# Second MoE by Winograd products: gate weights loaded a step earlier, output weights streamed for each pair of token blocks, one sum of z at a time, three output tiles

## The chip, the cores and the metric

The kernel runs on one core of one Trainium2 chip (one core, one launch). The metric is the device time of one execution in microseconds. Every profile here is one profiled execution of that one core. Engines are named as in the profile: PE multiplies, PEld loads its weights, DVE, ACT and POOL are the three elementwise engines, SP issues all DMAs.

## What is computed

The reference is a chunked attention followed by two feed-forward layers, all in fp32:

```python
x = attention(q, k, v, mem_k, mem_v)            # 4 x 768 tokens, 8 heads of 64 -> 3072 x 512
x = (np.maximum(x @ w_in, 0.0) ** 2) @ w_out    # first MoE: 512 -> 2048 -> 512
g = x @ w_gate                                  # second MoE: 512 -> 1536
out = (g / (1.0 + np.exp(-g)) * (x @ w_val)) @ w_out2    # 1536 -> 512
```

The weights arrive as float64; the kernel makes fp32 of them. An fp32 operand of a matmul is split in two parts, `hi` (rounded by ACT) and `lo` (the rest, by POOL or DVE), and each product is the sum of hi·hi, hi·lo and lo·hi.

## The kernel before

The program has two stages. Until about 629 us it does attention and the first MoE, in 8 blocks of 384 tokens and 16 slices of w1, with attention laid between. During that stage the second MoE's weights are turned into fp32, combined for the Winograd form and stored in two DRAM buffers, `w2g` (gate and value, 7 pieces for each of 12 slices f, L66) and `w2o` (output weights, two slices at a time, L67). The result of the first MoE goes to DRAM as `y1d`.

The change is in the second stage. It has 48 steps: 4 blocks s of 768 tokens, and for each the 12 slices f (`seq2`, L480). One step i is a call of `gated` (L417): seven products of 6 matmuls with 384 columns, L405, called A11, S2, A12, S3, S1, A22, S4. Each is read out of `hbank` by an ACT copy (L421) or a DVE operation (L425 to L449). Between them `fill` lays the 18 matmuls with 512 columns of `output` of the step before (L468). The results are combined by DVE L438 to L451 and ACT `Silu` (L430, L450), and rounded to `uh`, `ul` (L412 to L415), which the next step's `output` reads. PE's order is the order of the program. The other engines' instructions are ordered by a scheduler, within what the buffers allow.

What has to be ready for a step:
- its gate weights. `load_gv(i, half)` issues a DMA of 512 or 384 KB into a buffer of the tag "cut" (two buffers, `CB`, L32), `split_gv` casts it on ACT and subtracts on POOL, into a pair of buffers of the pool `wp`. Loads of step i+1 are put in slots 1 and 2 of step i, their splits in slots 3 and 5 (L580).
- the output weights. `load_out(c)`, `split_out(c)` bring the six pairs of slices in while s is 0; they stay in 12 of the 32 buffers of `wp` to the end (dictionary `wo`).
- z, the tokens of the block s in the forms that Winograd needs. `load_z` (L358) reads `y1d` into two buffers "raw"; `split_b1` splits B11 and B21 into the tile `z`; `sums_1` and `sums_2` form T1, T3, T2, T4 on POOL (L379, L380, L386, L387, 128x768 each); `split_t` splits the five forms into pairs of `wp` by halves of 384 columns. The forms of the next s are made in the last steps of the present one, four of the five in step 11 (L586 to L589).

`wp` has 32 buffers, 16 pairs. During the first MoE they hold w1 and come free as its last block uses them.

At f = 11 `output` finishes each of six tiles in turn, copies it to SBUF by ACT (L474) or DVE (L472) into one of two buffers "o" (L470) and stores it (L476).

The lines of the loads in the schedule, before the change:

```python
for slot, fn, half in ((1, load_gv, 0), (2, load_gv, 1), (3, split_gv, 0), (5, split_gv, 1)):
    job(i, slot, fn, i + 1, half)
if i % 2 == 0 and i // 2 + 1 < NF2 // 2:
    job(i, 6, load_out, i // 2 + 1)
    job(i + 1, 6, split_out, i // 2 + 1)
```

## Time and profile before

| | us |
|---|---|
| median of 3 runs | 1235.07 (1233.87 to 1235.35) |
| the profiled execution's own time | 1234.65 |
| its span, first to last instruction | 1232.8 |
| PE busy | 1164.0 |
| DVE busy | 690.4 |
| ACT busy | 593.5 |
| POOL busy | 320.3 |
| mean granted TensorE clock | 0.989 |

The span is 1.85 us shorter than the execution's own time; that rest lies around the span. The execution is 0.42 us below the median. Busy times of engines overlap, so they do not add up to the span; what an engine's idle time costs depends on whether the engine that ends last was waiting for it.

### The profile page before, as it was taken

How to read it: one execution, taken by the hardware profiler on the slowest of the kernel's cores; microseconds unless marked ns; L12 is line 12 of the kernel's file. 1: busy time of each engine (PE TensorE's matmuls, PEld its weight loads, DVE VectorE, ACT ScalarE, POOL GpSimd, SP SyncE). 2: the span in 40 equal slices, each digit the busy share in tenths (PEclk: the TensorE clock that was granted, in tenths of full speed). 3: DMA queues.
4: the chain of work that ended last, by engine and by line, in shares of the span. 5: the costliest groups of instructions: out<-in, count | busy, mean ns of one | idle time of the engine just before them, and what ended most of it. 6: DMA issues, size and time to landing. Idle time of an engine off the chain costs nothing.

```text
span 1232.8 us, 20450 instructions
## 1 busy us (share of the span) xinstructions
PE 1164.0 (94%) x8000; PEld 1099.2 (89%) x8000; DVE 690.4 (56%) x1251; ACT 593.5 (48%) x1510; POOL 320.3 (26%) x277
## 2 busy tenths in 40 slices
PE   2699999999999999999989999799997999999997
PEld 1599999999999999999988899699896998989896
DVE  7997345547365464532335555645566555665554
ACT  5686545546555554544743334434344333444422
POOL 0000000203011020002446533635335453345510
PEclk9999999999999999999989999899998999999999
DMA  7553205527244452501353122522225222143301
GB/s 269 195 207 117 75 25 173 193 70 273 81 150 147 137 210 80 181 1 69 95 166 95 60 77 77 192 66 68 77 61 192 73 61 90 61 146 103 103 1 51
DMA packets 46848, 140.77 MB, mean 114 GB/s; under 512 B 4512, under 2 KB 14240, under 8 KB 42400
## 3 DMA queue, kind: packets, MB, share of 16 engines
q1 hardware_dynamic: 46752, 139.48, 34.2%
q8 instruction: 62, 1.02, 0.3%
q14 instruction: 34, 0.28, 0.1%
HBM read 112.72 MB, written 26.74 MB: 113 GB/s over the span
## 4 chain that ended last, share of the span: by engine, by line
PE 80%; DVE 8%; DMA 5%; ACT 2%; POOL 2%; issue 2%; SPq 0%; ACTq 0%; DVEq 0%; POOLq 0%
PE hbank L405 25%; PE yb L295 19%; PE hbank L264 19%; PE yb L468 9%; PE abank L468 5%; PE abank L197 2%; POOL wlo L79 2%; DVE pT L178 2%; DMA wraw<-in_w_dram 2%; DMA gvraw<-w2g 1%; PE abank L136 1%; DMA out_dram<-o 1%; DVE wlo L79 1%; DVE cut L97 1%; ACT whi L76 1%
## 5 line engine op out<-in xcount | busy, mean ns | idle before, releaser
L79 POOL TENSOR_TENSOR wlo<-gvraw,whi 128x512 fp32r<-128x512 f32 x192 | 231.4, 1227 | 307.0 <-ACT whi L76 277.0
L264 PE MATMUL hbank<-x,whi 128*128 128x384 f32 x1024 | 200.0, 336 | 0.6 <-ACT x L76 0.6
L264 PEld LDWEIGHTS hbank<-x,whi 128*128 128x128 f32 x1024 | 180.5, 189 | 1.0 <-ACT x L76 0.9
L274 DVE TENSOR_TENSOR gl<-r,gh 128x384 fp32r<-128x384 f32 x128 | 75.1, 588 | 188.8 <-ACT r L273 188.4
L76 ACT CAST uh<-tmp 128x384 fp32r<-128x384 f32 x96 | 49.4, 514 | 191.8 <-DVE tmp L444 166.0
L328 POOL TENSOR_TENSOR wraw<-cut 128x256 f32<-128x256 f32 x24 | 19.8, 848 | 461.3 <-DVE mx L149 342.9
L405 PE MATMUL hbank<-whi 128*128 128x384 f32 x480 | 125.0, 342 | 9.0 <-DVE tmp L439 5.4
L271 ACT ACTIVATE r<-hbank 128x384 f32<-128x384 f32 x128 | 62.9, 491 | 143.2 <-PE hbank L264 142.0
L76 ACT CAST whi<-gvraw 128x512 fp32r<-128x512 f32 x192 | 100.0, 564 | 65.9 <-DMA gvraw<-w2g 38.1
L405 PE MATMUL hbank<-wlo,whi 128*128 128x384 f32 x480 | 125.3, 342 | 0.0
L405 PE MATMUL hbank<-whi,wlo 128*128 128x384 f32 x480 | 123.7, 338 | 0.0
L405 PEld LDWEIGHTS hbank<-whi 128*128 128x128 f32 x480 | 89.8, 190 | 33.0 <-DVE tmp L439 6.5
L295 PE MATMUL yb<-gh,whi 128*128 128x384 f32 x512 | 116.3, 341 | 0.0
L295 PE MATMUL yb<-gh,wlo 128*128 128x384 f32 x512 | 113.5, 335 | 0.0
L295 PE MATMUL yb<-gl,whi 128*128 128x384 f32 x512 | 113.3, 334 | 0.0
L264 PE MATMUL hbank<-x,wlo 128*128 128x384 f32 x512 | 109.6, 334 | 0.0
L178 DVE STREAM_TRANSPOSE pT<-prob 32x256 f32<-32x256 f32 x224 | 97.3, 435 | 3.6
L79 DVE TENSOR_TENSOR ul<-tmp,uh 128x384 fp32r<-128x384 f32 x96 | 66.7, 695 | 45.5 <-ACT uh L76 44.7
L295 PEld LDWEIGHTS yb<-gh,wlo 128*128 128x128 f32 x512 | 91.5, 188 | 0.0
L295 PEld LDWEIGHTS yb<-gh,whi 128*128 128x128 f32 x512 | 89.1, 188 | 2.5
L295 PEld LDWEIGHTS yb<-gl,whi 128*128 128x128 f32 x512 | 90.9, 188 | 0.1
L264 PEld LDWEIGHTS hbank<-x,wlo 128*128 128x128 f32 x512 | 90.7, 188 | 0.0
(92 smaller groups left out, 2042.2 us busy)
## 6 DMA issues: line engine op xcount, KB each, us to landing
wraw<-in_w_dram SPq DMA_DIRECT2D x34, 1024.0 KB, 6.2
gvraw<-w2g SPq DMA_DIRECT2D x48, 512.0 KB, 3.6
gvraw<-w2g SPq DMA_DIRECT2D x48, 384.0 KB, 3.1
qk<-in_att_dram SPq DMA_DIRECT2D x32, 464.0 KB, 4.4
v<-in_att_dram SPq DMA_DIRECT2D x32, 256.0 KB, 3.3
y1d<-ys SPq DMA_DIRECT2D x8, 768.0 KB, 3.8
w2g<-wraw SPq DMA_DIRECT2D x12, 512.0 KB, 3.9
zraw<-y1d SPq DMA_DIRECT2D x8, 768.0 KB, 5.1
```

The lines of the kernel that those rows point to most:

```text
L76: act.copy(hi, src)
L79: lo_engine.tensor_tensor(lo, src, hi.bitcast(F32), ALU.subtract)
L97: dve.scalar_tensor_tensor(w.bitcast(I32), upper, 3, lower, ALU.logical_shift_left, ALU.bitwise_or)
L178: dve.transpose(pT[row:row + 32, :, 32 * c:32 * c + 32], probs[u % 2][32 * c:32 * c + 32, :, col:col + 32],)
L197: pe.matmul(o[r:r + D, h // NI, h % NI // 2], s["v"][:, h * D:(h + 1) * D], pT[:, h], start=True, stop=True, tile_position=(0, r),)
L264: pe.matmul(hps, wt[:, k * 128:(k + 1) * 128], x[:, k, 0:n], start=i == 0, stop=i == 3 * KD - 1)
L271: act.activation(r, hps, AF.Relu)
L274: dve.tensor_tensor(gl, r, gh.bitcast(F32), ALU.subtract)
L295: pe.matmul(y[e], wt[:, c:c + 128], g, start=f == 0 and p == 0, stop=f == NF1 - 1 and p == 2)
L328: pool.tensor_tensor(o, x, y, op)
L405: pe.matmul(to, wt[:, k * 128:k * 128 + 128], z[:, k], start=n == 0, stop=n == 5)
L468: pe.matmul(outs[j], u[:, c:c + 128], wt, start=f == 0 and p == 0, stop=f == NF2 - 1 and p == 2)
```

## The change

Gate weights are loaded almost a step earlier: the loads of step i+1 are put in slots 4 and 7 of step i-1, the splits in slots 2 and 5 of step i. Two buffers "cut" serve only them, since the raw output weights and the temporary t2 now come from `wp` (`spare`). The output weights are no longer kept: they are loaded and split anew for every pair of steps, 24 times in place of 6. B1 is split in two jobs in two steps, sums and splits of z are one a step, and the split of a form is one ACT and one DVE job of 128x768 in place of two of 128x384. Tiles `o` are three. Line numbers behind the diff grow by 5 (L405 becomes L410, L421 becomes L426, L468 becomes L473); sums_1 is L385 and L386, sums_2 L392 and L393.

```diff
@@ -306,7 +306,7 @@
 
     NC2 = NF2 * 3 // 2
     WAT = {n: i * QC for i, n in enumerate(("A11", "A12", "S2", "S3", "S1", "S4", "A22"))}
-    w2t, wo = {}, {}
+    w2t = {}
 
     def load2(c):
         w["raw2", c] = load_w(w2[c])
@@ -330,28 +330,36 @@
         sp.dma_start(out=dst[:, 2 * QC:6 * QC], in_=sums)
         sp.dma_start(out=dst[:, 6 * QC:7 * QC], in_=a22)
 
-    def split_parts(hi, lo, src, n, step, lo_engine):
-        for c in range(0, n, step):
-            split(hi[:, c:c + step], lo[:, c:c + step], src[:, c:c + step], act, lo_engine)
+    def fetch(key, raw, src, n):
+        w["raw2", key] = raw[:, 0:n]
+        sp.dma_start(out=raw[:, 0:n], in_=src)
+
+    def split_w(key):
+        raw = w.pop(("raw2", key))
+        n = raw.shape[1]
+        w2t[key] = pair(wp, "w")
+        for c in (0, n // 2):
+            split(*(t[:, c:c + n // 2] for t in w2t[key]), raw[:, c:c + n // 2], act, pool)
+
+    def spare():
+        return wp.tile([128, WC], F32, tag="w", name="spare")
+
+    NGV = (4 * QC, 3 * QC)
 
     def load_gv(i, half):
-        n = (4 * QC, 3 * QC)[half]
-        w["gv", i, half] = rawp.tile([128, WC], F32, tag="cut", name="gvraw", bufs=CB)[:, 0:n]
         c = 4 * QC * half
-        sp.dma_start(out=w["gv", i, half], in_=w2g[seq2[i][1], :, c:c + n])
+        raw = rawp.tile([128, WC], F32, tag="cut", name="gvraw", bufs=CB)
+        fetch((i, half), raw, w2g[seq2[i][1], :, c:c + NGV[half]], NGV[half])
 
     def split_gv(i, half):
-        w2t[i, half] = pair(wp, "w")
-        n = (4 * QC, 3 * QC)[half]
-        split_parts(*w2t[i, half], w.pop(("gv", i, half)), n, n // 2, pool)
-
-    def load_out(c):
-        w["out", c] = rawp.tile([128, WC], F32, tag="cut", name="oraw", bufs=CB)
-        sp.dma_start(out=w["out", c], in_=w2o[c])
-
-    def split_out(c):
-        wo[c] = pair(wp, "w")
-        split_parts(*wo[c], w.pop(("out", c)), WC, 512, pool)
+        split_w((i, half))
+
+
+    def load_out(i):
+        fetch(("out", i), spare(), w2o[seq2[i][1] // 2], WC)
+
+    def split_out(i):
+        split_w(("out", i))
 
     zt, zraw = {}, {}
 
@@ -363,35 +371,32 @@
             sp.dma_start(out=z, in_=y1d[:, :, t0:t0 + NT2])
             zraw[s].append(z)
 
-    def split_z(s, name, hi, lo, src):
-        for k in range(2):
-            split(hi[:, k], lo[:, k], src[:, k], act, dve)
-        zt.setdefault(s, {})[name] = hi, lo
-
-    def split_b1(s):
-        hi, lo = [xp.tile([128, KD, NTM], R, tag=f"x{i}", name=f"z{i}") for i in range(2)]
-        for k in range(2):
-            split_z(s, ("B11", "B21")[k], *(t[:, 2 * k:2 * k + 2, 0:NT2] for t in (hi, lo)), zraw[s][0][:, 2 * k:2 * k + 2])
+    def split_b1(s, k):
+        if k == 0:
+            zt[s] = {}
+            zt[s]["x"] = [xp.tile([128, KD, NTM], R, tag=f"x{i}", name=f"z{i}") for i in range(2)]
+        rows = slice(2 * k, 2 * k + 2)
+        hi, lo = zt[s][("B11", "B21")[k]] = [t[:, rows, 0:NT2] for t in zt[s]["x"]]
+        split(hi, lo, zraw[s][0][:, rows], act, dve)
 
     def sums_1(s):
         z0, z1 = zraw[s]
         b11, b12, b22 = z0[:, 0:2], z1[:, 0:2], z1[:, 2:4]
         pool.tensor_tensor(b11, b12, b11, ALU.subtract)
         pool.tensor_tensor(b12, b22, b12, ALU.subtract)
+        zt[s].update(T1=b11, T3=b12, B22=b22)
 
     def sums_2(s):
         z0, z1 = zraw[s]
-        t1, b21, b22 = z0[:, 0:2], z0[:, 2:4], z1[:, 2:4]
-        t2 = rawp.tile([128, WC], F32, tag="cut", name="t2", bufs=CB)[:, 0:2 * NT2].rearrange("p (k n) -> p k n", k=2)
-        pool.tensor_tensor(t2, b22, t1, ALU.subtract)
-        pool.tensor_tensor(b21, t2, b21, ALU.subtract)
-        w["t2", s] = t2
+        t2 = spare()[:, 0:2 * NT2].rearrange("p (k n) -> p k n", k=2)
+        pool.tensor_tensor(t2, z1[:, 2:4], z0[:, 0:2], ALU.subtract)
+        pool.tensor_tensor(z0[:, 2:4], t2, z0[:, 2:4], ALU.subtract)
+        zt[s].update(T2=t2, T4=z0[:, 2:4])
 
     def split_t(s, name):
-        z0, z1 = zraw[s]
-        src = w.pop(("t2", s)) if name == "T2" else {"T1": z0[:, 0:2], "T4": z0[:, 2:4], "T3": z1[:, 0:2], "B22": z1[:, 2:4]}[name]
-        hi, lo = (t[:, 0:2 * NT2].rearrange("p (k n) -> p k n", k=2) for t in pair(wp, "w"))
-        split_z(s, name, hi, lo, src)
+        src = zt[s][name]
+        zt[s][name] = [t[:, 0:2 * NT2].rearrange("p (k n) -> p k n", k=2) for t in pair(wp, "w")]
+        split(*zt[s][name], src, act, dve)
 
     utile = {}
 
@@ -457,7 +462,7 @@
 
     def output(i):
         s, f = seq2[i]
-        hi, lo = (t[:, f % 2 * DM:f % 2 * DM + DM] for t in wo[f // 2])
+        hi, lo = (t[:, f % 2 * DM:f % 2 * DM + DM] for t in w2t["out", i // 2 * 2])
         order = [(3 * b + j, p) for b in range(2) for p in range(3) for j in range(3)]
         if f == NF2 - 1:
             order = [(j, p) for j in range(6) for p in range(3)]
@@ -467,7 +472,7 @@
             c = 128 * (j % 3)
             pe.matmul(outs[j], u[:, c:c + 128], wt, start=f == 0 and p == 0, stop=f == NF2 - 1 and p == 2)
             if f == NF2 - 1 and p == 2:
-                o = up.tile([128, DM], F32, tag="o", name="o", bufs=2)
+                o = up.tile([128, DM], F32, tag="o", name="o", bufs=3)
                 if j % 2:
                     dve.tensor_copy(o, outs[j])
                 else:
@@ -506,10 +511,11 @@
         at(a - 8, load2, c)
         at(a, prep2, c)
     for f, fn, *args in (
-        (0, load_z, 0), (2, split_b1, 0), (3, sums_1, 0), (4, sums_2, 0), (5, split_t, 0, "T2"),
-        (6, split_t, 0, "T3"), (7, split_t, 0, "T1"), (8, split_t, 0, "T4"), (9, split_t, 0, "B22"),
-        (9, load_gv, 0, 0), (10, load_gv, 0, 1), (11, split_gv, 0, 0), (12, split_gv, 0, 1),
-        (12, load_out, 0), (14, split_out, 0),
+        (0, load_z, 0), (2, split_b1, 0, 0), (3, split_b1, 0, 1), (3, sums_1, 0), (4, sums_2, 0),
+        (4, split_t, 0, "T2"), (5, split_t, 0, "T3"), (6, split_t, 0, "T1"), (6, load_gv, 0, 0), (7, split_t, 0, "T4"),
+        (7, load_gv, 0, 1), (8, split_t, 0, "B22"), (9, load_out, 0), (9, split_gv, 0, 0), (10, split_gv, 0, 1),
+        (11, load_gv, 1, 0), (12, split_out, 0), (12, load_gv, 1, 1), (13, split_gv, 1, 0), (14, split_gv, 1, 1),
+        (14, load_out, 2),
     ):
         at(last + 4 * f + 2, fn, *args)
     lookahead = 2
@@ -576,16 +582,21 @@
             jobs.setdefault((i, slot), []).append((fn, args))
 
     for i, (s, f) in enumerate(seq2):
-        if i + 1 < len(seq2):
-            for slot, fn, half in ((1, load_gv, 0), (2, load_gv, 1), (3, split_gv, 0), (5, split_gv, 1)):
-                job(i, slot, fn, i + 1, half)
-        if i % 2 == 0 and i // 2 + 1 < NF2 // 2:
-            job(i, 6, load_out, i // 2 + 1)
-            job(i + 1, 6, split_out, i // 2 + 1)
+        if i > 0:
+            if i + 1 < len(seq2):
+                job(i - 1, 4, load_gv, i + 1, 0)
+                job(i - 1, 7, load_gv, i + 1, 1)
+                job(i, 2, split_gv, i + 1, 0)
+                job(i, 5, split_gv, i + 1, 1)
+        if i % 2 == 0 and i + 2 < len(seq2):
+            if i > 0:
+                job(i, 7, load_out, i + 2)
+            job(i + 1, 3, split_out, i + 2)
         if f == 0 and i + NF2 < len(seq2):
             for at_f, slot, fn, *args in (
-                (3, 4, load_z), (5, 4, split_b1), (6, 4, sums_1), (7, 4, sums_2), (8, 4, split_t, "T2"),
-                (11, 4, split_t, "T3"), (11, 5, split_t, "T1"), (11, 6, split_t, "T4"), (11, 7, split_t, "B22"),
+                (2, 2, load_z), (4, 4, split_b1, 0), (5, 4, split_b1, 1), (6, 1, sums_1), (6, 4, sums_2),
+                (7, 4, split_t, "T2"), (8, 4, split_t, "T3"), (9, 4, split_t, "T1"), (10, 4, split_t, "T4"),
+                (11, 3, split_t, "B22"),
             ):
                 job(i + at_f, slot, fn, s + 1, *args)
     todo = iter(())
```

How the scheduler's order moves with it, at three places.

POOL around T1 and T3 of z for s = 2, in step 12 before and step 11 after (names carry buffer numbers; the rows `wlo<-gvraw` are halves of splits of gate weights, `x2` two of them). Before:

```order
L79 TENSOR_TENSOR wlo_7836<-gvraw_7804,whi_7835 128x512 x2
L79 TENSOR_TENSOR wlo_7869<-gvraw_7819,whi_7868 128x384 x2
L379 TENSOR_TENSOR zraw_8169<-zraw_8171,zraw_8169 128x768
L380 TENSOR_TENSOR zraw_8171<-zraw_8171 128x768
L79 TENSOR_TENSOR wlo_7950<-gvraw_7924,whi_7949 128x512 x2
L79 TENSOR_TENSOR wlo_7977<-gvraw_7936,whi_7976 128x384 x2
```

With the change:

```order
L79 TENSOR_TENSOR wlo_7802<-gvraw_7723,whi_7801 128x512 x2
L385 TENSOR_TENSOR zraw_8028<-zraw_8030,zraw_8028 128x768
L386 TENSOR_TENSOR zraw_8030<-zraw_8030 128x768
L79 TENSOR_TENSOR wlo_7851<-gvraw_7772,whi_7850 128x384 x2
L79 TENSOR_TENSOR wlo_7921<-gvraw_7834,whi_7920 128x512 x2
L79 TENSOR_TENSOR wlo_7938<-spare_7892,whi_7937 128x512 x2
L79 TENSOR_TENSOR wlo_7967<-gvraw_7894,whi_7966 128x384 x2
```

The two sums now stand in front of the 128x384 split of gate weights of step 13. Two rows on, a split of output weights (`spare`) stands in front of the 128x384 split of step 14.

ACT around the copy that opens step 12 (L450, L421 before are L455, L426 after; `z` is the tile of B11 and B21). Before:

```order
L76 CAST whi<-zraw 128x384 x4
L76 CAST whi<-gvraw 128x512 x2
L76 CAST whi<-gvraw 128x384
L76 CAST uh<-tmp 128x384
L76 CAST whi<-gvraw 128x384
L450 ACTIVATE tmp<-tmp 128x384
L76 CAST z_8377<-zraw 128x384
L421 COPY tmp<-hbank_75 128x384
L76 CAST uh<-tmp 128x384
L76 CAST z_8377<-zraw 128x384 x2
L474 COPY o<-yb_78 128x512
```

With the change:

```order
L76 CAST whi<-gvraw 128x384 x2
L76 CAST whi<-gvraw 128x512 x2
L76 CAST uh<-tmp 128x384
L76 CAST whi<-spare 128x512 x2
L76 CAST whi<-gvraw 128x384
L455 ACTIVATE tmp<-tmp 128x384
L426 COPY tmp<-hbank_75 128x384
L76 CAST whi<-gvraw 128x384
L76 CAST uh<-tmp 128x384
L76 CAST whi<-gvraw 128x512
L479 COPY o<-yb_78 128x512
```

One cast of gate weights of step 14, 128x384, stands directly in front of the Silu and of the copy that opens step 12, behind two casts of output weights.

DVE in step 0 (L425 to L449 read `hbank`; the row L79 z is the split of B11 or B21 of s = 1). Before:

```order
L434 TENSOR_TENSOR tmp<-hbank_76,tmp 128x384
L79 TENSOR_TENSOR z_7065<-zraw,z_7064 128x384
L438 TENSOR_TENSOR tmp<-hbank_75,tmp 128x384
L439 TENSOR_TENSOR tmp<-hbank_75,tmp 128x384
L443 TENSOR_TENSOR tmp<-tmp,hbank_76 128x384
L79 TENSOR_TENSOR z_7065<-zraw,z_7064 128x384
L444 TENSOR_TENSOR tmp<-tmp 128x384
L449 TENSOR_TENSOR tmp<-hbank_75,tmp 128x384
```

With the change:

```order
L439 TENSOR_TENSOR tmp<-hbank_76,tmp 128x384
L79 TENSOR_TENSOR z_6947<-zraw,z_6946 128x768
L443 TENSOR_TENSOR tmp<-hbank_75,tmp 128x384
L444 TENSOR_TENSOR tmp<-hbank_75,tmp 128x384
L448 TENSOR_TENSOR tmp<-tmp,hbank_76 128x384
L79 TENSOR_TENSOR z_6947<-zraw,z_6946 128x768
L449 TENSOR_TENSOR tmp<-tmp 128x384
L454 TENSOR_TENSOR tmp<-hbank_75,tmp 128x384
```

The first of these splits, of B11, stands in the same place, ahead of the two operations on the product S1 (L438, L439 before, L443, L444 after), and is one row of 128x768.

## Rows read from the trace of the kernel before

**Rows 1.** Page, part 1: busy time, share of the span, instructions of PE, PEld, DVE, ACT, POOL
```profile
PE 1164.0 (94%) x8000; PEld 1099.2 (89%) x8000; DVE 690.4 (56%) x1251; ACT 593.5 (48%) x1510; POOL 320.3 (26%) x277
```

**Rows 2.** Timeline of ACT: start us, us, of the L421 copies of steps 0, 3, 11, 14, 15
```profile
630.99 0.49 ACT L421 COPY tmp<-hbank 128x384 f32<-128x384 f32 x1
...
671.14 0.46 ACT L421 COPY tmp<-hbank 128x384 f32<-128x384 f32 x1
...
765.47 0.46 ACT L421 COPY tmp<-hbank 128x384 f32<-128x384 f32 x1
...
811.65 0.47 ACT L421 COPY tmp<-hbank 128x384 f32<-128x384 f32 x1
823.25 0.47 ACT L421 COPY tmp<-hbank 128x384 f32<-128x384 f32 x1
```

**Rows 3.** The same for steps 23, 26, 35, 37 and 47
```profile
917.08 0.46 ACT L421 COPY tmp<-hbank 128x384 f32<-128x384 f32 x1
...
962.17 0.47 ACT L421 COPY tmp<-hbank 128x384 f32<-128x384 f32 x1
...
1067.67 0.46 ACT L421 COPY tmp<-hbank 128x384 f32<-128x384 f32 x1
...
1094.55 0.46 ACT L421 COPY tmp<-hbank 128x384 f32<-128x384 f32 x1
...
1211.23 0.47 ACT L421 COPY tmp<-hbank 128x384 f32<-128x384 f32 x1
```

**Rows 4.** Waits of PE, 605 to 1233 us: us in total, times, longest us
```profile
PE yb L468 <- ACT o L474: 6.6, 2, 3.3
PE abank L468 <- DVE o L472: 5.5, 2, 3.0
PE hbank L405 <- DVE tmp L439: 5.4, 1, 5.4
PE hbank L405 <- DVE tmp L449: 1.9, 2, 1.4
```

**Rows 5.** Windows: us, busy of PE, PEld, DVE, ACT, POOL; clock, DMA share, GB/s
```profile
780.00:800.00 20.00, 13.69 (x64) 11.55 (x63) 12.56 (x21) 8.85 (x18) 11.72 (x8) 0.84 0.60 193
800.00:820.00 20.00, 20.00 (x96) 18.60 (x95) 8.56 (x16) 5.87 (x12) 6.83 (x6) 0.90 0.21 64
```

**Rows 6.** Timeline of POOL, SP and ACT in step 12
```profile
782.47 2.10 POOL L379 TENSOR_TENSOR zraw<-zraw 128x768 f32<-128x768 f32 x1 [2.57 <-DVE z L79]
786.67 5.11 POOL L79 TENSOR_TENSOR wlo<-gvraw,whi 128x512 fp32r<-128x512 f32 x4
...
789.56 0.33 SPq L341 DMA_DIRECT2D gvraw<-w2g  x1
...
793.87 0.62 ACT L76 CAST whi<-gvraw 128x512 fp32r<-128x512 f32 x1 [4.94 <-DMA gvraw<-w2g]
...
795.92 0.47 ACT L421 COPY tmp<-hbank 128x384 f32<-128x384 f32 x1
```

**Rows 7.** Timeline of SP and DVE in step 0
```profile
632.61 0.58 SPq L363 DMA_DIRECT2D zraw<-y1d  x1
...
639.69 0.65 DVE L79 TENSOR_TENSOR z<-zraw,z 128x384 fp32r<-128x384 f32 x1 [5.22 <-ACT z L76]
```

**Rows 8.** Timeline of DVE and POOL in step 5
```profile
702.57 1.62 DVE L444 TENSOR_TENSOR tmp<-tmp 128x384 f32<-128x384 f32 x1
...
709.68 0.56 DVE L79 TENSOR_TENSOR ul<-tmp,uh 128x384 fp32r<-128x384 f32 x1 [0.58 <-ACT uh L76]
...
701.93 1.85 POOL L386 TENSOR_TENSOR t<-zraw 128x768 f32<-128x768 f32 x1
```

**Rows 9.** Groups by form, 640 to 1233 us: POOL's splits of output weights
```profile
L79 POOL TENSOR_TENSOR wlo<-oraw,whi 128x512 fp32r<-128x512 f32 x8 | 10.8, 1366 | 5.0 <-ACT whi L76 5.0
```

**Rows 10.** Page, part 6: loads of the second half of gate weights
```profile
gvraw<-w2g SPq DMA_DIRECT2D x48, 384.0 KB, 3.1
```

**Rows 11.** Timeline of ACT: its last copy of o
```profile
1228.29 0.59 ACT L474 COPY o<-yb 128x512 f32<-128x512 f32 x1 [2.15 <-DMA out_dram<-o]
```

## The prediction

> **What bounds the kernel now.** I read the page's busy times first, then the starts of the copies that open each step (L421), then PE's waits and the windows around the longest ones, and last the timelines of POOL, SP, ACT and DVE there. PE is busy 94% of the span, no other engine over 56% [rows 1], so a gain must come out of PE's waits or out of the clock. A step with no wait lasts 823.25 - 811.65 = 11.60 us [rows 2]. Step 0 has no `output` to lay in: 18 x 512 of 25,344 columns less, by my estimate 7.3 us. From the copy of step 0 to that of step 47, 630.99 to 1211.23 us [rows 2, 3], 7.3 + 46 x 11.60 = 540.9 of the 580.24 us are work; 39.3 us are excess. The starts put it in few places:
> - A, steps 0 to 2 (630.99 to 671.14): 40.15 - 7.3 - 23.2 = 9.65.
> - B1, steps 11 to 13 (765.47 to 811.65): 46.18 - 34.8 = 11.38.
> - B2, steps 23 to 25 (917.08 to 962.17): 10.29.
> - B3, steps 35 and 36 (1067.67 to 1094.55): 26.88 - 23.2 = 3.68.
> - M, all other steps together: 4.34 (1.5, 1.0, 1.1 and 0.7 in the four stretches between those places, each its length less 11.60 us a step).
>
> The reader is to see in B1, in step 12, a chain over four engines. POOL forms T1 of z for s = 2 (2.10 us), then T3, then does four weight splits (5.11 us) [rows 6]; only then is a buffer "cut" free and SP issues the next gate load, at 789.56. ACT waits 4.94 us for its data with a cast at the head of its queue [rows 6]. Behind that cast stand an output copy, the Silu and the copy of step 13, which starts at 795.92. PE waits for output copies on ACT and DVE, 6.6 and 5.5 us in two times each over B1 and B2 [rows 4]. After the wait the granted clock is below full: 0.84 and then 0.90 over 20 us [rows 5], though in the second window PE is never idle. So a wait costs more than its length.
>
> **A, step 0.** The load of z is issued at 632.61 and the split of B11 stands ahead of L438 and L439 on DVE, idle 5.22 us before it [rows 7]; PE waits 5.4 us for L439 [rows 4]. In the new order that split is in the same place. It is one operation of 128x768 in place of two of 128x384, so DVE holds L443 some 0.5 us more; on SP the load stands behind gate loads of step 4, freed, by my estimate, 1 us earlier than the load is issued now. The ends are A as it is (9.65) and A without PE's wait (about 4.3). I take 9.0, near the first, since the order keeps the cause.
>
> **B1 and B2.** B11 and B21 of s = 2 go into the tile that s = 0 used, which is free after the product A12 of step 11. In the new orders that split and T1, T3 come at once, in step 11, so some 7 us earlier than now, but the split of step 13's second half stands behind them on POOL. The load of step 14's second half waits for that split, and its cast stands in ACT's queue directly ahead of the Silu and the copy that opens step 12. I count from step 11's opening copy. With A12 done and the casts and subtractions of B11 and B21 behind it, T1 starts by my estimate at 7.2. Two sums take 4.2 (2.10 each) [rows 6]. Two half splits of 384 columns take 2.0, at three quarters of 5.11 / 4 [rows 6]. The load takes 3.1 [rows 10], the cast 0.5, the Silu 0.5. The copy of step 12 so starts at 7.2 + 4.2 + 2.0 + 3.1 + 0.5 + 0.5 = 17.5. It is due at 11.6, and PE has by its columns some 1.3 us of other work (S2 and four output matmuls, less the copy itself). That leaves 17.5 - 12.9 = 4.6 us of wait. Before, PE's waits for output copies in B1 were half of 6.6 + 5.5, 6.05 us [rows 4], and the excess 11.38; the other 5.3 are smaller waits and matmuls at the lower clock. I keep 3.0 for the clock: 0.16 of the first window's 20 us [rows 5] is 3.2. A late `uh` and the next copy add 0.7, from the small waits on L449 and the like (1.4 at most) [rows 4]. B1 and B2 become 8.3 each: gains of 3.1 and 2.0. Bounds: 0 if the load is early enough; 12 if it stays and two output-weight casts (0.62 each, by the 0.62 us of a 128x512 cast [rows 6]) and a missing output copy stand in front too.
>
> **B3.** No z is made here; the burst of loads when T buffers come free remains, with one load fewer to hold. I take 3.2 for 3.68.
>
> **Output weights streamed.** 18 loads of 512 KB more, 36 POOL splits and 36 ACT casts of 128x512. POOL's take 1.37 us each [rows 9]: 36 x 1.37 = 49 us on an engine that works 320 of 1232.8 us [rows 1]. ACT's take 0.62 [rows 6]: 22 us on one that works 593.5. Both have room, so what counts is where they stand. A DVE operation with both operands in SBUF pays: L444 took 1.62 us while POOL ran T2 (701.93 to 703.78) [rows 8], against 0.56 us for a split of `ul` seven us later, with POOL idle [rows 8]. When a hold of this kind comes late in a step, PE waits for L449: 1.9 us in two times, 1.4 at most [rows 4]. The other end is 0: steps 1 to 9 hold five such output splits already and all of M in steps 3 to 10 is 1.5 us, of which T2 and T4 in step 5 explain the 1.4. I take near 0, since those are the same operations. M keeps its sums (T2 and T4 still wait for the product S3 of a step, and then hold `ul` and L454): 4.5 for 4.34.
>
> The Trainium skill, "SBUF — State Buffer", section "SBUF: two separate sides", says that DVE (with two SBUF inputs) and GpSimd take their shared port pair for a whole instruction, and that the other then blocks fully. The trace agrees: 1.62 against 0.56 us. By that rule alone every added split would block such a DVE operation for up to 1.4 us, which is the slower rival below.
>
> **Loads in the first stage.** On SP the gate loads of step 0 now stand ahead of the last attention loads, which they delay by some 2 us; those loads are needed several us later. I take 0.
>
> **Tail.** With two tiles the last ACT copy of o waited 2.15 us for a store [rows 11]. With three it can follow its matmul. I take 2.1 off the end; the ends are 0 and 2.15.
>
> **The sum.** 0.65 (A) + 3.1 (B1) + 2.0 (B2) + 0.5 (B3) - 0.2 (M) + 2.1 (tail) = 8.15 us. It stands against the profiled execution's 1234.65: 1226.5 us. That execution lies 0.42 below the median of 1235.07, so against the median the same sum gives 1226.9. I forecast 1226.5. A measurement of this kernel can tell some 0.2%, or 2.5 us, from no change.
>
> **Rival 1, the boundaries empty.** If a gate load a step ahead is enough for ACT never to wait on it at the boundaries, B1, B2 and B3 go with their half-speed matmuls: 11.38 + 10.29 + 3.68 = 25.4, and with A and the tail 28: 1206.5. For it: the loads are moved almost a whole step of 11.60, more than the 4.94 us that ACT waited [rows 6]. Against it: with two buffers a load waits for the split of the load before it, wherever the program names it, and in the new order that split is still behind the sums. Half of it (only one of the chains goes) gives some 1216.
>
> **Rival 2, POOL's splits push DVE (slower).** The mechanism is in step after step: the 18 added output splits run in slot 3 or later, and if they fall between L444 and L454, `ul` waits and L454 with it, which the first product of the next step needs. Price: 0.95 us each, the mean of the two waits on L449 [rows 4]: 18 x 0.95 = 17 us, and 1234.65 - 8.15 + 17 = 1243.6. It decides from the point at which POOL begins the split later than about 8 us after the opening copy. For it: L444's 1.62 us [rows 8]. Against it: five such splits in steps 1 to 9 cost next to nothing.
>
> **Rival 3, no change.** Boundaries keep their 11 us, because more casts stand in front of the Silu, and only the tail gains: 1234.65 - 2.1 = 1232.6, to 1236 with little waits in M.
>
> **How the numbers follow.** Forecast (1217 to 1231): 0.46. Rival 1, fully or half: 0.18. Rival 3: 0.15, of which a little is still faster. Rival 2 or longer boundaries: 0.21. Faster by over 0.2% (below 1232.6) 0.65, within 0.2% 0.14, slower 0.21. The range that leaves out 2 in 10 goes from 1209 (most of rival 1 inside its half) to 1239 (half of rival 2).
>
> **What would show it.** Right: A's wait for L444 stays near 5 us; at steps 11 and 23 ACT still waits for a gate load, 3 to 6 us, in front of L455; steps between stay at 11.60; the last copies no longer wait for stores. Wrong: a copy L426 of step 12 less than 13 us behind that of step 11 (rival 1); steps of over 12 us in many odd places with PE waiting for L454 (rival 2); a window of low clock where there was none.

## The result and the profile after

The change is slower: 1248.23 us (median of 4 runs, 1243.13 to 1251.61) against 1234.78 for the kernel before (1233.87 to 1235.35), a ratio of 1.0106 with a 95% interval of 1.0068 to 1.0144. The forecast was 1226.5, in a range of 1209 to 1239. The profiled execution took 1246.47 us, 11.8 more than that of before.

The busy times of the page (PE, PEld, DVE, ACT, POOL), to be held against [rows 1]:

```profile
PE 1168.9 (94%) x8000; PEld 1101.3 (88%) x8000; DVE 718.2 (58%) x1223; ACT 608.5 (49%) x1518; POOL 376.1 (30%) x313
```

PE does the same 8000 matmuls. POOL has 36 instructions and 56 us more, ACT 15 us more. As before, no engine but PE is near its limit. Where the 11.8 us are is seen in the opening copies, now L426 (timeline of ACT; start us, us; the first is step 0, then 11 and 12, 14, and 38 to 40), against [rows 2, 3]:

```profile
631.50 0.48 ACT L426 COPY tmp<-hbank 128x384 f32<-128x384 f32 x1 [0.16 <-PE hbank L410]
...
766.37 0.48 ACT L426 COPY tmp<-hbank 128x384 f32<-128x384 f32 x1
785.62 0.46 ACT L426 COPY tmp<-hbank 128x384 f32<-128x384 f32 x1
...
810.52 0.46 ACT L426 COPY tmp<-hbank 128x384 f32<-128x384 f32 x1
...
1117.14 0.47 ACT L426 COPY tmp<-hbank 128x384 f32<-128x384 f32 x1
1130.22 0.46 ACT L426 COPY tmp<-hbank 128x384 f32<-128x384 f32 x1
1141.51 0.46 ACT L426 COPY tmp<-hbank 128x384 f32<-128x384 f32 x1
```

Read like before, with 11.60 us a step and 7.3 for step 0, the excess of each stretch is the difference of two such starts less its steps. All runs of the study are read that way (the last row is the time from the opening copy of step 47 to the end of the span):

| excess, us | before | change | output weights kept | before, 3 tiles o | 4 own pairs | kept at the boundaries |
|---|---|---|---|---|---|---|
| A, steps 0 to 2 | 9.7 | 10.1 | 8.0 | 8.6 | 6.5 | 5.7 |
| steps 3 to 10 | 1.5 | 1.5 | 1.0 | 1.8 | 0.6 | 0.6 |
| B1, 11 to 13 | 11.4 | 9.4 | 7.1 | 7.7 | 11.9 | 7.6 |
| 14 to 22 | 1.0 | 3.0 | 0.5 | 0.9 | 0.4 | 1.0 |
| B2, 23 to 25 | 10.3 | 11.9 | 7.1 | 6.8 | 13.1 | 7.0 |
| 26 to 34 | 1.1 | 3.0 | 0.5 | 1.0 | 1.4 | 1.3 |
| B3, 35 and 36 | 3.7 | 8.5 | 5.0 | 3.1 | 8.3 | 4.9 |
| 37 to 46 | 0.7 | 5.4 | 0.6 | 0.6 | 3.4 | 7.1 |
| last copy to the end | 21.6 | 19.7 | 19.5 | 19.5 | 19.7 | 19.6 |

The change gained 2.0 us at B1 and 1.9 in the tail. It lost 8.5 us in the steps away from the boundaries (1.0, 1.1 and 0.7 became 3.0, 3.0 and 5.4; 1.9 of the last is step 37, still behind B3), 1.6 at B2 and 4.8 at B3. PE's waits from 605 us on (total, times, longest), where [rows 4] stood:

```profile
PE hbank L410 <- DVE tmp L454: 13.8, 17, 1.5
PE yb L473 <- ACT uh L76: 6.3, 6, 1.5
PE hbank L410 <- DVE tmp L444: 5.9, 3, 5.3
PE hbank L410 <- ACT tmp L426: 5.8, 3, 3.7
```

The wait for L454, the operation that was L449, went from 1.9 us in 2 times to 13.8 in 17. Step 38 shows one of them (timelines of POOL, DVE and PE; in brackets the idle time before an instruction and what ended it):

```profile
1125.95 2.86 POOL L79 TENSOR_TENSOR wlo<-gvraw,whi 128x512 fp32r<-128x512 f32 x2 [7.92 <-issue]
1128.80 2.82 POOL L79 TENSOR_TENSOR wlo<-spare,whi 128x512 fp32r<-128x512 f32 x2
...
1126.05 1.61 DVE L449 TENSOR_TENSOR tmp<-tmp 128x384 f32<-128x384 f32 x1
1128.23 0.99 DVE L79 TENSOR_TENSOR ul<-tmp,uh 128x384 fp32r<-128x384 f32 x1 [0.58 <-ACT uh L76]
1129.15 0.55 DVE L454 TENSOR_TENSOR tmp<-hbank,tmp 128x384 f32<-128x384 f32 x1
...
1129.75 0.62 PE L410 MATMUL hbank<-whi 128*128 128x384 f32 x2 [0.88 <-DVE tmp L454]
```

POOL has stood idle for 7.92 us and only then splits gate weights, and behind them the output weights. Its 5.7 us of work lie on L449 (1.61 us; 0.56 in step 44, where POOL is idle) and on `ul` (0.99, there 0.56), and DVE comes to L454 late; PE waits 0.88 us. The steps 38, 40 and 42 all take 13.08 us, each with this wait, and the odd ones between them 11.29, so a pair costs 1.2 us more than two steps of 11.60. Steps 2, 14 and 26 have the same 0.88.

Why POOL is late: its buffer. In step 14 the profile names an output matmul on `abank` as what ends POOL's 7.92 us. The compiled program makes the 128x512 split of gate weights in step 14 wait for the output matmuls of step 13, which PE runs during step 14, because the pool `wp` hands that split the buffer of the streamed pair that those matmuls read. Twelve splits of the program wait for output matmuls; not each of them costs time: in step 16 ACT waits 4.63 us for one before a cast, and the step lasts 11.30 us.

At B1 the chain is the one forecast (timelines of POOL, SP and ACT in steps 11 and 12):

```profile
773.83 2.55 POOL L385 TENSOR_TENSOR zraw<-zraw 128x768 f32<-128x768 f32 x1
...
780.80 7.49 SPq L335 DMA_DIRECT2D gvraw<-w2g  x3
...
779.23 1.13 ACT L76 CAST whi<-spare 128x512 fp32r<-128x512 f32 x2
784.78 0.51 ACT L76 CAST whi<-gvraw 128x384 fp32r<-128x384 f32 x1 [4.42 <-DMA gvraw<-w2g]
785.20 0.52 ACT L455 ACTIVATE tmp<-tmp 128x384 f32<-128x384 f32 x1
```

T1 starts 7.5 us after the opening copy at 766.37, the load of step 14's second half is issued at 780.80, ACT waits 4.42 us for it with the Silu and the next opening copy behind. At B3 the clock is new. In the change PE is busy for 16.28 of the 20 us from 1080 on, and behind them the granted clock is 0.50, the lower of its two levels, from 1101.8 to 1108.6. A window of 20 us of the changed kernel over the end of step 36 and step 37 (columns as in [rows 5]), and the one of before that holds most of its step 36 and the start of 37:

```profile
1100.00:1120.00 20.00, 17.74 (x77) 16.29 (x78) 10.85 (x17) 8.35 (x18) 11.39 (x10) 0.83 0.47 152
```

```profile
1080.00:1100.00 20.00, 18.26 (x91) 16.15 (x92) 12.82 (x21) 10.68 (x22) 9.92 (x9) 1.00 0.62 193
```

### The profile page after: what moved, and what is told of

Same layout as the page of the kernel before. It is cut to its first block, busy times and chain, and to the rows that moved or that the text cites. A ratio compares the mean times of both kernels' runs of the same rounds, so it can differ in the third digit from the quotient of the medians.

```text
span 1244.7 us, 20548 instructions
## 1 busy us (share of the span) xinstructions
PE 1168.9 (94%) x8000; PEld 1101.3 (88%) x8000; DVE 718.2 (58%) x1223; ACT 608.5 (49%) x1518; POOL 376.1 (30%) x313
## 4 chain that ended last, share of the span: by engine, by line
PE 78%; DVE 8%; DMA 5%; POOL 3%; ACT 2%; issue 2%; SPq 0%; DVEq 0%; POOLq 0%; ACTq 0%
PE hbank L410 24%; PE yb L295 19%; PE hbank L264 19%; PE yb L473 9%; PE abank L473 4%; POOL wlo L79 3%; DMA wraw<-in_w_dram 3%; PE abank L197 2%; DMA gvraw<-w2g 2%; DVE pT L178 2%; PE abank L136 1%; DVE tmp L449 1%; DVE ul L79 1%; DVE cut L97 1%; ACT uh L76 1%
## 5 line engine op out<-in xcount | busy, mean ns | idle before, releaser
L79 POOL TENSOR_TENSOR wlo<-gvraw,whi 128x512 fp32r<-128x512 f32 x192 | 233.7, 1239 | 247.4 <-ACT whi L76 122.7
L274 DVE TENSOR_TENSOR gl<-r,gh 128x384 fp32r<-128x384 f32 x128 | 79.2, 620 | 182.8 <-ACT r L273 182.3
L410 PE MATMUL hbank<-whi 128*128 128x384 f32 x480 | 126.5, 345 | 19.9 <-DVE tmp L454 13.8
L410 PEld LDWEIGHTS hbank<-whi 128*128 128x128 f32 x480 | 89.2, 190 | 47.0 <-DVE tmp L454 20.0
L410 PE MATMUL hbank<-wlo,whi 128*128 128x384 f32 x480 | 126.3, 344 | 0.0
L410 PE MATMUL hbank<-whi,wlo 128*128 128x384 f32 x480 | 124.7, 341 | 0.0
L79 DVE TENSOR_TENSOR ul<-tmp,uh 128x384 fp32r<-128x384 f32 x96 | 77.4, 806 | 48.2 <-ACT uh L76 46.0
L410 PE MATMUL hbank<-z,whi 128*128 128x384 f32 x384 | 86.1, 347 | 5.8 <-ACT tmp L426 5.8
```

Of the source, the lines that this page charges most:

```text
L79: lo_engine.tensor_tensor(lo, src, hi.bitcast(F32), ALU.subtract)
L274: dve.tensor_tensor(gl, r, gh.bitcast(F32), ALU.subtract)
L410: pe.matmul(to, wt[:, k * 128:k * 128 + 128], z[:, k], start=n == 0, stop=n == 5)
```

## The experiments

In short, the runs show that streaming costs 25.3 us. A part of it comes from buffers that come free late, and a larger part stands at the changes of s. Theory 1: it is the late buffer; POOL's splits run when PE frees a buffer, and streaming makes that moment fall on DVE's late operations. Theory 2: it is the number of added POOL splits, wherever they run. Theory 3: it is the added traffic. Each kernel was timed against the kernel before on the same chip; that one's medians in these comparisons were 1234.9 to 1235.2.

**Output weights kept.** The change, with `load_out` and `split_out` doing nothing from s = 1 on:

```diff
     def load_out(i):
-        fetch(("out", i), spare(), w2o[seq2[i][1] // 2], WC)
+        if i < NF2:
+            fetch(("out", i), spare(), w2o[seq2[i][1] // 2], WC)
...
-        hi, lo = (t[:, f % 2 * DM:f % 2 * DM + DM] for t in w2t["out", i // 2 * 2])
+        hi, lo = (t[:, f % 2 * DM:f % 2 * DM + DM] for t in w2t["out", f // 2 * 2])
```

> The change, but the output weights are loaded and split once (six pairs, while s is 0) and kept, as before. Against the profiled execution before, the changed one is 11.8 us longer: +8.6 in the steps away from the boundaries (4.3 to 12.9 us of excess over 11.60 a step), +4.8 at steps 35 and 36, +1.6 at 23 to 25, -2.0 at 11 to 13, about +0.9 at the start, -2.0 in the tail. Theory 1 (streaming, by the buffers): a streamed pair of output weights is freed only by the output matmuls late in an even step, POOL's split of gate weights takes that buffer and so runs late, and DVE's L449 and ul are held by it. Then keeping the weights brings the steps away from the boundaries back to 3 to 5 us and steps 35, 36 to 3 to 5: 1231 to 1236 us. Theory 2 (the added POOL splits hold DVE wherever they stand) expects the same here. Rival (the loss comes from the earlier gate loads and the new order of z, not from streaming): no change, 1243 to 1250 us.

1222.95 us, ratio to before 0.9896 (0.9879 to 0.9913): faster than expected, and faster than the kernel before. Streaming alone costs 25.3 us of 1248.23. PE's waits (L446 and L456 are that kernel's L439 and L449 of before):

```profile
PE hbank L412 <- DVE tmp L446: 4.7, 2, 4.5
PE hbank L412 <- DVE tmp L456: 3.4, 5, 1.1
```

POOL's splits in steps 14 to 16:

```profile
815.49 2.87 POOL L79 TENSOR_TENSOR wlo<-gvraw,whi 128x512 fp32r<-128x512 f32 x2 [3.68 <-ACT whi L76]
821.42 1.99 POOL L79 TENSOR_TENSOR wlo<-gvraw,whi 128x384 fp32r<-128x384 f32 x2 [3.06 <-ACT whi L76]
827.02 2.86 POOL L79 TENSOR_TENSOR wlo<-gvraw,whi 128x512 fp32r<-128x512 f32 x2 [3.61 <-ACT whi L76]
```

They start 10.6 us after an opening copy (128x512) and 5.0 after it (128x384), step after step; by the program, what holds each is the product that last read its buffer, S4 or S3. At these moments DVE is past `ul`, or reads PSUM, which POOL does not slow (in step 38, L454 took 0.55 us beside a POOL split). In the change the 128x512 split starts at 8.8 in steps 14, 26, 38, 40 and 42.

**The lo parts of output weights on DVE.**

```diff
-    def split_w(key):
+    def split_w(key, lo_engine=pool):
...
-        split_w(("out", i))
+        split_w(("out", i), dve if i >= NF2 else pool)
```

> The change, but from s = 1 on the lo parts of the output weights are subtracted on DVE in place of POOL, so POOL has no added split left; the buffers and their waits stay. Theory 1 (late buffer): POOL's gate split still waits for the output matmuls in steps 14, 26, 38, 40, 42 and still holds L449 and ul, so PE's 0.88 us waits for L454 stay there, and the time stays at 1243 to 1250 us. Theory 2 (the number of added POOL splits): those waits go, excess away from the boundaries falls from 12.9 to 4 to 6 us, 1237 to 1241 us.

1239.17 us (1233.54 to 1242.83 in ten runs), ratio 1.003 (1.0013 to 1.0047), 9 below the change. The time is the one of theory 2, the waits in step 38 are those of theory 1; both have part of it. Step 38 has not moved (POOL, PE):

```profile
1121.91 2.86 POOL L79 TENSOR_TENSOR wlo<-gvraw,whi 128x512 fp32r<-128x512 f32 x2 [7.92 <-PE abank L473]
...
1125.71 0.63 PE L410 MATMUL hbank<-whi 128*128 128x384 f32 x2 [0.88 <-DVE tmp L454]
```

The split waits 7.92 us for the output matmul and PE 0.88 us for L454, with no added split on POOL; steps 14, 26, 38, 40 and 42 take 13.08 us as before, as theory 1 said. But the boundaries and the last stretch fell by 5.4 us in sum (B1 0.7, B2 1.1, B3 1.4, the last 2.2): there the work on POOL counts. This profiled execution took 1242.79 us, only 3.7 less than that of the change, so where the rest of the 9 us lies is not shown.

**Two pairs of their own for the streamed weights.** A tag of its own with 4 buffers, 28 for the rest:

```diff
-        return [pool_.tile([128, 1024], R, tag=tag, name=n) for n in ("whi", "wlo")]
+        return [pool_.tile([128, 1024], R, tag=tag, name=n, bufs=4 if tag == "wa" else 28) for n in ("whi", "wlo")]
...
-        w[f] = pair(wp, "w")
+        w[f] = pair(wp, "wa" if f < 2 else "w")
...
-        w2t[key] = pair(wp, "w")
+        w2t[key] = pair(wp, "wa" if key[0] == "out" else "w")
...
```

> The change, but the pool wp is parted: 28 buffers as before and 4 of a tag of their own, which hold w1's first two slices and then only the streamed pairs of output weights. The same loads, casts and POOL splits remain. Theory 1 (late buffer): gate splits no longer wait for the output matmuls, POOL's idle 7.9 us ahead of them goes, PE's 0.88 us waits in steps 14, 26, 38, 40, 42 go, excess away from the boundaries falls from 12.9 to 4 to 7 us: 1237 to 1242 us. Theory 2 (number of POOL splits) and theory 3 (9.4 MB more of DRAM traffic): no change, 1243 to 1250 us.

1279.01 us, ratio 1.0346 (1.0322 to 1.0369): far on the wrong side, for theory 1 as I had put it too. The edit did not take the late buffer away. With two pairs, the next streamed pair needs the pair whose last reader is the output matmul that ends an even step, and 22 splits of the compiled program now wait for output matmuls, in place of 12. PE's waits, and an operation of DVE in step 17 that comes late:

```profile
PE hbank L410 <- ACT tmp L426: 23.0, 12, 3.3
PE hbank L410 <- DVE tmp L430: 13.3, 6, 2.3
PE hbank L410 <- DVE tmp L454: 12.6, 16, 1.6
```

```profile
865.42 0.96 DVE L79 TENSOR_TENSOR wlo<-spare,whi 128x768 fp32r<-128x768 f32 x1 [2.42 <-POOL wlo L79]
```

In step 16 ACT waited 2.85 us for an output matmul before the cast of a streamed pair, with `uh` and the Silu queued behind, but that step still lasted 11.26 us. The loss is in step 17, 16.44 us: POOL splits the streamed pair only then, DVE's split of a form of z (T2, in a `spare`) comes 2.42 us late behind POOL, and PE waits 2.18 us for L430 behind it. What a late buffer costs depends on what stands behind it. The largest sum, 23.0 us for the copies that open a step, was not followed back wait by wait.

**Three tiles o in the kernel before**, one number changed (L470, 2 to 3).

> The kernel before with three tiles o in place of two and nothing else. By the prediction's tail term, and by the tail of the changed kernel (1225.04 to 1244.7 us, 19.7 us from the last opening copy to the end, against 21.6 before): 2.0 us less, 1232.5 to 1233.2 us; more, up to 6 us less, if the output copies at steps 12 and 24 were also waiting for a tile (PE waited 6.6 and 5.5 us for them). Rival (the boundaries wait for the gate load and not for o, and the tail is bound by the stores): within 0.5 us of before.

1224.87 us, ratio 0.9915 (0.9897 to 0.9933): 10.3 us from one buffer, more than the 6 at most that I had expected. The tail gives the expected 2.1 (21.6 to 19.5); B1 and B2 give 3.6 and 3.5. The wait for ACT's o, 6.6 us in [rows 4], is gone; what is left:

```profile
PE abank L468 <- DVE o L472: 6.2, 2, 3.2
PE hbank L405 <- DVE tmp L439: 5.1, 1, 5.1
```

Step 12 shows how (SP and ACT of before, then ACT with three tiles):

```profile
789.93 0.43 SPq L476 DMA_DIRECT2D out_dram<-o  x1
794.49 0.58 ACT L474 COPY o<-yb 128x512 f32<-128x512 f32 x1
```

```profile
789.09 0.59 ACT L474 COPY o<-yb 128x512 f32<-128x512 f32 x1 [0.59 <-PE yb L468]
```

The store issued at 789.93 landed at 794.42 and freed the tile that the copy of 794.49 writes. The cast in front of that copy, which waits for the gate load, ended at the same moment, so one wait hid the other. At B2 it is the same: 945.96 and 946.04. With three tiles the copy stands ahead of that cast, 8.1 us behind the opening copy of step 12 and not 15.0.

**Traffic alone.** To the kernel with kept weights, a DRAM-to-DRAM copy of each pair that streaming would load:

```diff
...
+        else:
+            sp.dma_start(out=copy[seq2[i][1] // 2], in_=w2o[seq2[i][1] // 2])
...
```

> The kernel with resident output weights (1222.95 us), and in each pair of steps from s = 1 on a copy of 512 KB of the output weights from DRAM to another place in DRAM, 18 in all: the added loads without a buffer, a cast or a split. Theory 3 (the added traffic delays the gate loads on which ACT waits at the boundaries): 1230 to 1240 us, gate loads landing later than 3.6 and 3.1 us. Theories 1 and 2: 1222 to 1225 us.

1224.29 us, 1.3 more than without. But the run does not test theory 3: nothing held the copies back, and they ran in the first stage, the last of them at 527.5 us (all 18 copies: ns of issuing, lowest, median and highest; first and last start in us):

```profile
L363 SPq DMA_DIRECT2D copy<-w2o x18: 467/474/1853, 231.3 to 527.5; - x18
```

What bears on theory 3 are the gate loads of the change itself, beside the streamed ones. They land in the median as fast as without streaming, and their 384 KB as fast as before [rows 10] (page of the change, part 6: KB each, us to landing):

```profile
gvraw<-w2g SPq DMA_DIRECT2D x48, 512.0 KB, 3.5
gvraw<-w2g SPq DMA_DIRECT2D x48, 384.0 KB, 3.1
```

The longest landing is 5.9 us in the change and 5.8 with kept weights. Nothing here points at the traffic, but no run has it alone in the second stage.

**POOL work alone.** To the kernel with kept weights, two subtractions into an unread tile behind every second gate split:

```diff
+        if n == WC and key[0] != "out" and key[0] >= NF2 and key[0] % 2 == 0:
+            for c in (0, n // 2):
+                junk = up.tile([128, n // 2], F32, tag="junk", name="junk", bufs=1)
+                pool.tensor_tensor(junk, raw[:, c:c + n // 2], w2t[key][1][:, n // 2:n].bitcast(F32), ALU.subtract)
```

> The kernel with resident output weights (1222.95 us), and behind POOL's split of the first half of gate weights of every even step from s = 1 on two more subtractions of 128x512 into a tile that nobody reads: 36 of them, as many as streaming adds, without loads, casts or buffers of wp. In that kernel POOL's splits stand at 10.6 and 0.3 us after the copy that opens a step, so the added ones should run at about 1.6 to 4.1, where DVE has one operation with both operands in SBUF (ul) to hold. Theory 2 (the number of added POOL splits, 0.95 us each): 1240 us. Theory 1 (it depends on where they run, and the late buffer puts them on L449, ul and L456): 1223 to 1227 us.

1233.97 us, 11 over the kernel with kept weights, between the two expectations: theory 1 was too low, theory 2 too high. The place decides (POOL in steps 15 and 16, and at B2):

```profile
830.61 2.87 POOL L79 TENSOR_TENSOR wlo<-gvraw,whi 128x512 fp32r<-128x512 f32 x2 [3.61 <-ACT whi L76]
833.55 2.86 POOL L346 TENSOR_TENSOR junk<-gvraw,wlo 128x512 f32<-128x512 f32 x2
...
941.65 1.27 POOL L346 TENSOR_TENSOR junk<-gvraw,wlo 128x512 f32<-128x512 f32 x1
942.88 1.31 POOL L79 TENSOR_TENSOR wlo<-gvraw,whi 128x384 fp32r<-128x384 f32 x1
```

In the two middle stretches the added work stands at 2.0 and 3.5 us after the opening copy, in steps 18 and 30 at 6.8 and 8.1, and the excess is 0.47 and 0.50 us, as without it: nothing. B1, B2 and B3 lost 3.4, 2.4 and 2.0 us, the last stretch 2.8. At B1 to B3 the added work runs at 8.5 to 12 us in steps 11, 23 and 35 and at 10 to 17 us in the steps behind them, there in front of a split that a gate load is waiting for. In step 39, in the last stretch, it holds `ul` (0.98 us). One thing sets this run apart from streaming: the added subtractions read the gate weights' raw buffer, so the next load has to wait for them (SP waited 18 times for one, 108.4 us in sum), while streaming's splits read a buffer of `wp`. What they cost at the boundaries is therefore not exactly the price of streaming's splits.

**Streaming in the kernel before**, through its own two buffers "cut" and with two tiles o:

```diff
-        sp.dma_start(out=w["out", c], in_=w2o[c])
+        sp.dma_start(out=w["out", c], in_=w2o[c % (NF2 // 2)])
...
-        hi, lo = (t[:, f % 2 * DM:f % 2 * DM + DM] for t in wo[f // 2])
+        hi, lo = (t[:, f % 2 * DM:f % 2 * DM + DM] for t in wo[i // 2])
...
-        if i % 2 == 0 and i // 2 + 1 < NF2 // 2:
+        if i % 2 == 0 and i + 2 < len(seq2):
```

> The kernel before with the output weights streamed for each pair of steps, in its own slots 6, through its two buffers cut, and two tiles o as before: streaming alone. Compiled, its output splits wait for the output matmuls that end a step. Theory 1 and the run with resident weights (streaming costs 24 us): 1248 to 1262 us, with PE waits for the late DVE operations or for the opening copy in every second step. Rival (streaming costs only together with the earlier gate loads): 1234 to 1239 us.

1298.83 us, ratio 1.0519 (1.0491 to 1.0547), worse than either expectation. Here the raw output weights take one of the two buffers that the gate loads need, and ACT waits for gate loads again and again, here in step 37, where no z is made:

```profile
1148.20 1.14 ACT L76 CAST whi<-gvraw 128x512 fp32r<-128x512 f32 x2 [4.91 <-DMA gvraw<-w2g]
1154.61 0.93 ACT L76 CAST whi<-gvraw 128x384 fp32r<-128x384 f32 x2 [3.73 <-DMA gvraw<-w2g]
```

Streaming through these two buffers costs 63.7 us here; through `wp`, in the change, 25.3. The two schedules differ in more than that, so the gap is not the buffers' alone.

**Z a step later**, to remove A, in the kernel with kept weights:

```diff
-                (2, 2, load_z), (4, 4, split_b1, 0), (5, 4, split_b1, 1), (6, 1, sums_1), (6, 4, sums_2),
+                (3, 2, load_z), (5, 1, split_b1, 0), (5, 6, split_b1, 1), (6, 1, sums_1), (6, 4, sums_2),
```

> The kernel with resident output weights (1222.95 us) with the jobs of z for the next block a step later: load in step 3 of a block, splits of B11 and B21 in slots 1 and 6 of step 5. Compiled, DVE's split of B11 of s = 1 no longer stands ahead of L445 and L446 in step 0. If that split is what PE waits 4.5 us for there: that wait goes with its half-clock window, excess of steps 0 to 2 from 7.95 to 2 to 4 us, 1217 to 1219 us. Rival (the queue behind moves the wait to step 1, or the products of step 0 wait for the load anyway): 1222 to 1224 us.

1222.37 us, no difference from 1222.95 that can be told. The wait in step 0 is gone and A falls from 8.0 to 2.7 us, but step 0 opens at 635.91 in place of 630.69. 1.82 us of that is a new wait for the first copy, which stands behind a cast of gate weights (PE in step 0):

```profile
636.43 0.98 PE L412 MATMUL hbank<-z,whi 128*128 128x384 f32 x4 [1.82 <-ACT tmp L428]
```

The rest lies in the first stage, which ends 1 to 5 us later in several of the other profiled executions too (630.7 to 635.9); whether that belongs to this edit stays open.

**Four pairs of their own**, the run with two pairs mended: 8 buffers and 24, with w1's first four slices in the 8. The edit is that of two pairs with these numbers.

> The change with wp parted 24 and 8: four pairs of their own for the streamed output weights, so that each pair is reused only four pairs of steps later. Compiled, no split in the program waits for an output matmul any more (12 do in the change, 22 in the run with two pairs of their own). All loads, casts and POOL splits of streaming remain. Theory 1 (late buffer): the steps away from the boundaries come back to 1 to 3 us of excess in each of the two long stretches (2.99 now) and the last stretch from 5.4 to under 3; what remains is the work of the splits at the boundaries, where the run with added POOL work lost 8 us: 1230 to 1239 us. If the work, wherever it stands, is what costs: 1245 to 1255 us. If parting the pool is itself what made the run with two own pairs slow: 1265 to 1285 us.

1239.9 us, ratio 1.0046 (1.0031 to 1.0061): 8.3 below the change with all of streaming's loads, casts and splits, and just outside the 1230 to 1239 of theory 1. No split waits for an output matmul. The stretch of steps 14 to 22 has 0.4 us of excess, the other two 1.4 and 3.4, so with steps 3 to 10 the steps away from the boundaries have 5.9 us and not 12.9; A is 3.5 us shorter too. POOL in step 15:

```profile
821.49 2.55 POOL L79 TENSOR_TENSOR wlo<-spare,whi 128x512 fp32r<-128x512 f32 x2 [6.36 <-ACT whi L76]
824.12 4.50 POOL L79 TENSOR_TENSOR wlo<-gvraw,whi 128x512 fp32r<-128x512 f32 x4
830.92 2.85 POOL L79 TENSOR_TENSOR wlo<-gvraw,whi 128x512 fp32r<-128x512 f32 x2 [2.30 <-ACT whi L76]
```

None of them has waited for an output matmul. PE's waits:

```profile
PE hbank L410 <- ACT tmp L426: 8.0, 6, 2.6
PE hbank L410 <- DVE tmp L454: 3.3, 4, 1.3
```

The wait for L454 is down from 13.8 us to 3.3. Parting the pool is not what made the run with two pairs slow. The boundaries are no better: 11.9, 13.1 and 8.3, for 9.4, 11.9 and 8.5 in the change. 17 of the 25.3 us that streaming costs are still there.

**Gate loads back in their old slots**, in the kernel with kept weights:

```diff
-                job(i - 1, 4, load_gv, i + 1, 0)
-                job(i - 1, 7, load_gv, i + 1, 1)
-                job(i, 2, split_gv, i + 1, 0)
+                job(i, 1, load_gv, i + 1, 0)
+                job(i, 2, load_gv, i + 1, 1)
+                job(i, 3, split_gv, i + 1, 0)
```

> The kernel with resident output weights (1222.95 us), with the loads and splits of gate weights put back in the slots of the kernel before (loads in slots 1 and 2, splits in 3 and 5 of the step before their use). If the earlier loads bring something by themselves: 1226 to 1232 us, boundaries longer by 1 to 3 us each. If, as the compiled waits say, a load is set by when its buffer cut comes free and not by its slot: 1222 to 1225 us.

1226.33 us (1223.87 to 1229.11), 3.4 more. B1 and B2 are shorter and B3 is 0.3 longer (6.5, 6.6 and 5.3 for 7.1, 7.1 and 5.0); the profiled execution is longer at the start of the stage (step 0 opens 4.5 us later, A has 2.9 more). So at the boundaries the earlier slots bring nothing; what they bring at the start cannot be told from the first stage's own spread.

**Two tiles o in the change**, three to two.

> The change with two tiles o as before in place of three. In the kernel before, the third tile alone brought 10.3 us, 3.6 and 3.5 of it at the boundaries and 2.1 in the tail. If it brings the same inside the change: 1256 to 1262 us. If streaming hides the wait for it at the boundaries: 1249 to 1253 us (the tail alone).

1250.68 us (1248.87 to 1254.12), 2.45 more than the change, whose own four runs lie 8.5 us apart. The tail is 2.0 us longer (21.7 us for 19.7), where the last ACT copy waits for a store again:

```profile
1244.17 0.58 ACT L479 COPY o<-yb 128x512 f32<-128x512 f32 x1 [2.16 <-DMA out_dram<-o]
```

In the tail the third tile is worth what I had put down for it, 2.1 us. Whether that is all in the change is not shown: in this profile B1 and B2 are 2.9 and 1.3 us longer too, and the last stretch 1.5 shorter. It is far from the 10.3 in the kernel before.

**Nothing streamed at the boundaries**: four own pairs, slices 0 to 3 kept in `wp`.

```diff
...
     def load_out(i):
-        fetch(("out", i), spare(), w2o[seq2[i][1] // 2], WC)
+        if i < NF2 or i % NF2 > 3:
+            fetch(("out", i), spare(), w2o[seq2[i][1] // 2], WC)
...
-        w2t[key] = pair(wp, "wa" if key[0] == "out" else "w")
+        w2t[key] = pair(wp, "wa" if key[0] == "out" and key[1] > 3 else "w")
...
-        hi, lo = (t[:, f % 2 * DM:f % 2 * DM + DM] for t in w2t["out", i // 2 * 2])
+        hi, lo = (t[:, f % 2 * DM:f % 2 * DM + DM] for t in w2t["out", (f if f < 4 else i) // 2 * 2])
```

> The run with four pairs of its own for streamed output weights (1239.9 us), but the weights of slices 0 to 3 are kept in two pairs of wp, so that nothing is streamed in the steps around a change of s; slices 4 to 11 are streamed as there. 12 of 18 added loads and 24 of 36 added splits remain. That run loses 4.8, 6.0 and 3.3 us at the three boundaries against the kernel with resident weights, and 3.8 in the steps between. If the added casts and splits in front of the Silu, the opening copy and the sums are what costs there: boundaries at 7 to 8, 7 to 8 and 5 us, 1225 to 1231 us. If the boundaries lose by the order of z or the parted pool and not by the splits: 1236 to 1241 us.

1229.2 us, ratio 0.9959 (0.9942 to 0.9975). The boundaries are back to 7.6, 7.0 and 4.9 us, those of the kernel with kept weights. 6.3 us over the kernel with kept weights remain. They lie in steps 38 to 41; in step 40 a gate load for which ACT waits with the Silu behind:

```profile
1135.80 0.62 ACT L76 CAST whi<-gvraw 128x512 fp32r<-128x512 f32 x1 [3.71 <-DMA gvraw<-w2g]
1136.33 0.52 ACT L457 ACTIVATE tmp<-tmp 128x384 f32<-128x384 f32 x1
```

## Why the prediction was wrong

The step that failed is "Output weights streamed", where I took near 0. In its place the runs show a cost of 25.3 us (1248.23 with streaming, 1222.95 without). The argument was that five such splits in steps 1 to 9 cost nothing, and that the new ones are the same operations. The old ones still cost nothing there: 1.5 us in steps 3 to 10 before and after. Two things do not carry over. One is when POOL runs: a split cannot start before the buffer that it is handed is free, and streaming hands gate splits buffers that output matmuls of the step before have to free. With four own pairs 8.3 us go, and no split waits for such a matmul. The other is where the added work stands: I counted none of it at the boundaries, and keeping it off them, in the last run, takes another 10.7 us (1239.9 to 1229.2). The last 6.3 us show at gate loads of steps 38 to 41; why those come late stays open.

Point by point:
- **M**, forecast 4.5, measured 12.9. The late buffer has the larger part: with four own pairs, all work kept, it is 5.9, and steps 14 to 22 fall from 3.0 to 0.4 us. Rival 2 had the mechanism on DVE: a POOL split between what are now L449 and L454 holds `ul` (it names the first by its old number, L444). Its time, 1243.6, lies 4.6 us under what was measured. But it had another cause. In step 38 the gate split, moved by the buffer, comes first, and with no added split on POOL PE's 0.88 us stay; the 16 of 36 added subtractions that run in the two middle stretches cost nothing. Its 0.95 us were 0.88, in six steps and not in 18, and the rest of the loss is elsewhere.
- **B1**, forecast 8.3, measured 9.4: right in chain for the change and nearly in size. Without streaming that chain is short (step 11 takes 13.87 us, not 17.5), so the 8.3 is in part luck. The copy of step 12 came 19.25 us after that of step 11, against 17.5 forecast, chiefly because T1 took 2.55 us and the load 3.98 from issue to cast. And in the kernel before, the two ACT copies at B1 and B2 for which PE waited 6.6 us had been waiting for their tile as well.
- **B2** 8.3 and **B3** 3.2, measured 11.9 and 8.5. The streamed splits are missing from both terms. Without streaming they are 7.1 and 5.0; with streaming kept off the steps around a change of s, 7.0 and 4.9. At B3 a stretch of half clock is new.
- **A**, forecast 9.0, measured 10.1: the cause stayed, as the order said (PE waits up to 5.3 us for L444), and the gain of 0.65 us did not come.
- **Tail**, forecast 2.1, measured 1.9, and 2.0 the other way when the third tile is taken out of the change: right. But the same tile alone brings 10.3 us in the kernel before, since the ACT copies at steps 12 and 24 also wait for a free tile. I saw 6.6 and 5.5 us of waits for output copies there and put them down to the gate load. The 6.6 us go with a third tile; of the wait for DVE's copies 6.2 us remain.
- **The rule on the shared port pair** (the Trainium skill, "SBUF — State Buffer", "SBUF: two separate sides"), beside which rival 2 stood, agrees with step 38: L449 took 1.61 us under POOL's split. By itself the rule gives a price and no place; in step 38 the price was not what I lacked.
- The forecast's sum, 8.15 us of gain, is not far from what the change brings without streaming, 12.2. That is luck: it holds 2.1 us for the tile, which alone brought 10.3 in the kernel before, and 6 for the rest.
